# New due times for the keys, the first queries and the logits in an attention-plus-experts kernel

## The chip, the core and the metric

The kernel runs on one core of one Trainium2 chip. The metric is the device time of one execution in microseconds (us), as the median of several runs. TensorE does the matmuls, VectorE and ScalarE read their results out of PSUM, GpSimd takes some subtractions and the indirect transfers, and SyncE's queue issues nearly all DMAs. In the rows of the profile these are PE (PEld for weight loads), DVE, ACT, POOL and SP.

## What is computed

Four batches of 11456 tokens with 128 channels, 49 agents for each batch, and 8 experts of width 1024. Cut to what matters:

```python
def sm(a, b):                                   # softmax over the last axis
    s = scale * (a @ b.transpose(0, 2, 1))
    s = s - s.max(-1, keepdims=True)
    e = np.exp(s)
    return e / (e.sum(-1, keepdims=True) + 1e-09)
agent_v = sm(agents, k) @ v                     # 49 x 128 for each batch
x = sm(q, agents) @ agent_v                     # tokens x 128
logits = x @ w_gate                             # 8 experts
expert_idx = np.argmax(logits, axis=1)
gate = softmax(logits)[expert_idx]
out[t] = gate[t] * (relu(x[t] @ w1[e]) @ w2[e]) # e = expert_idx[t]
```

## The kernel before

A batch is cut into 12 chunks: eleven of 1024 tokens (128 partitions of 8 tokens) and one of 192. Every fp32 operand is split into a high and a low f16 part, so that three f16 matmuls stand for one fp32 matmul.

**The expert work** of a batch is 23 groups of 512 tokens (the last one smaller) by 8 tiles of the hidden width, which makes 184 turns of the generator `experts`, called steps here. A step writes one `ph` tile with two matmuls (`layer1`, lines 1204 and 1205), ScalarE and VectorE turn it into `hh` (lines 1210 and 1211), and five steps later (`LAG`) twelve matmuls of `layer2` (line 1224) read that `hh`. Four `ph` tiles in PSUM let TensorE run ahead of VectorE by a few steps. The first layer reads `M`, the transposed exponentials of a query chunk; 16 steps use one chunk. One expert is chosen for a whole batch (`choose`), and its weights are folded with the agent values into `Ah` and `Al` and split into `w2h` and `w2l` (`weights`, with the small chain of `pow2_scale`, lines 185 to 197). Tokens of other experts are gathered and redone in blocks near the end.

**The attention work** is laid between these steps. For each chunk `prepare` sums squares (line 332), splits the loaded tile into `hl` (ScalarE line 360, VectorE line 362) and lets SyncE issue a DMA transposition into `hT` (line 387). Then
- the keys of the next batch go through `kscores` (lines 415 to 417, ScalarE copies the scores to `S` in line 433) and `kmax` (VectorE `mx`, line 452), all 12 chunks before the values may start;
- the queries of the batch go through `qscores` (VectorE `mq` and `E`, lines 616 and 618), `qexp` (ScalarE, then a store `exps`), `esplit` three steps later (VectorE or GpSimd `mm`, lines 630 and 634), and a DMA transposition into `M` (line 640);
- `logits` (line 649) multiplies `M` by the gating weights, VectorE reduces the result into `Ld` (line 651), and `route` and `factors` make from it the gate that `store` needs.

Scores, logits, values and all small matmuls share two PSUM tiles (`psS`).

**What sets the order.** Each piece of work is an event with a due time in steps, counted from the start of the batch that it belongs to; a heap hands the events out in the order of these times, and the code that they call is written into the program in that order. Each engine then works through its own list in order, and the compiler's tile layer may shift a row by a few places. The due times come from the numbers at the top of the file. `KS` and `KT` are the first key chunk and the steps between chunks: -208 is 24 steps ahead of the batch before (184 steps). `QA` and `QB` do the same for the first three query chunks, `QC` (13 steps) for the rest. `KL` is the distance from preparing a chunk to its scores, `LL` from scores to logits, and `KLL`, `LLL` are these two for the last batch. Step numbers in this document are (batch, step), both from 0. A chunk of keys is named by the batch whose keys they are.

Of the kernel before, what the change touches and what calls it, by code (L numbers as in the profile page):

```python
# [45 lines left out]
KS0, KT0, KL0, VT0, VL0, QS0, QT0, QL0 = -200, 2, 4, 2, 1, -146, 3, 5  # L46
VE, T1, TF0, TF1, TL, TLM, Q0 = 12, 1.75, 3, 1.5, 18, 10, 2

KS, KT, VT, VL, VL4, TW0, TW1, DW = -208, 9, 5.3, 8, 5, 8, 2.5, 1
QA, QB, QC, QB3, KL, LL, UD, RG, D1, DL = -20, 8, 13, 10.5, 9, 9.5, 2, 0.7, 0.5, 0  # L50

KS1 = []

KLL, LLL = 11, 11

DTR, DTE, DEX, DST, DXS = 2, 0.5, 2, 2, 0.5

# [13 lines left out]
def agent_moe_kernel(ctx, tc, q, k, v, agents, wg, w1, w2, out):  # L71
# [185 lines left out]
    def at(t, f, *a):  # L257
        count[0] += 1
        heapq.heappush(events, (t, count[0], f, a))
# [4 lines left out]
    def turns(gen, t, dt, n):  # L264
        for i in range(n):
            at(t + i * dt, next, gen, None)
# [3 lines left out]
    def attention(b):  # L270
        st = state[b]
        base = b * steps
        first, last = b == 0, b + 1 == B
# [492 lines left out]
        def use(t, src, c):  # L766
            uses.append((base + t, b, src, c))

        def prepare(t, src, c):
            at(base + t, squares, src, c)  # L770
            at(base + t + (0 if first else D1), total, src, c)
            at(base + t + (0.5 if first else UD), total2, src, c)
            at(base + t + (1 if first else D1 + 0.3 if src != "v" else UD + 1), transposed if how[src, c] == "C" else split, src, c)
# [6 lines left out]
        for c in range(NCK):  # L780
            t = KS1[c] - base if b == 1 and c < len(KS1) else ks + kt * c
# [8 lines left out]
        for c in range(NCK):  # L790
            t = tv + vt * c
# [21 lines left out]
        for c in range(NCK):  # L813
            if first and c < NQ:
                t, ql_ = QS0 + QT0 * c, QL0
            else:
                t = (Q0 + QC * (c - 3) if first and c > 2 else QA + QB * c if c < 3 else
                     QA + 2 * QB + (QB3 if last else QC) * (c - 2))
                ql_ = KLL if last and c > 2 else KL
            use(t, "q", c)  # L820
            prepare(t, "q", c)
            at(base + t + ql_, qscores, c)
            at(base + t + ql_ + (0 if first and c < NQ else DL), qexp, c)
            at(base + t + ql_ + 3, esplit, c)
            tl = max(t + ql_ + (TL if first and c < NQ else LLL if last and c > 2 else LL), ta + (TLM if first else 4) + c / 2)
            at(base + tl, logits, c)
            if c + 1 in starts or c == NCK - 1:
                turns(route(c), base + tl + 1, RG, 6)
                tf = max(tl + 1 + 6 * RG, tw + 1)
                at(base + tf, factors, c)  # L830
                c0 = max(x for x in starts if x <= c)
                assert tf < c0 * 16 + LAG + 8, (b, c, tf)
# [444 lines left out]
    for b in range(B):  # L1277
        attention(b)
        turns(experts(b), b * steps, 1, steps + LAG + 2)
        turns(leftover_ranks(b), b * steps + (LT3 if b + 1 == B else LT), LTS3 if b + 1 == B else LTS, 6)  # L1280
# [92 lines left out]
```

## Time and profile before

| | |
|---|---|
| three runs | 1165.85, 1166.04 and 1166.94 us, median 1166.04 |
| profiled execution | 1163.97 us |
| its span, first to last instruction | 1162.2 us |
| PE, DVE, ACT, POOL busy | 1028.1, 1016.7, 840.4, 231.5 us |
| mean granted TensorE clock | 0.961 of full speed |

The expert steps run from 85.6 us (the first matmul of line 1204) to 1104.1 us (the last). What stands ahead is the first batch's attention, what follows are the gathered blocks. Batches begin at 85.6, 357.9, 612.9 and 862.9 us. A busy share tells little here, since the two busiest engines wait on each other through four PSUM tiles; what counts is in which step TensorE stands still, for whom, and whether VectorE had work left in that time.

### The profile page before, as it was taken

To read this page: it belongs to the slowest core of one execution; us is meant where nothing else is said; L and a number is where in the kernel's file an instruction comes from. 1 tells how busy PE (TensorE), PEld (TensorE's weight loads), DVE (VectorE), ACT (ScalarE), POOL (GpSimd) and SP (SyncE) were. 2 spreads that over 40 slices of the span, in tenths; PEclk is the share of its full clock that TensorE was granted. 3 is DMA by queue.
4 is the path that set the end of the run, shared out by engine and by line. 5 is a ranking of instruction groups with operands and counts; after the bars stand their busy time and mean duration, and the time that the engine had idled before them with its cause. 6 is when DMAs were issued, how large, how long until landed. Compare 5 with 4: busy or idle time off the path is not lost. (4 is left out here: it accounts for less than half of the span.)

```text
span 1162.2 us, 36038 instructions
## 1 busy us (share of the span) xinstructions
PE 1028.1 (88%) x14607; PEld 827.9 (71%) x14607; DVE 1016.7 (87%) x2407; ACT 840.4 (72%) x1506; POOL 231.5 (20%) x369
## 2 busy tenths in 40 slices
PE   6757789988989989989988889999989988989895
PEld 5645668767867777777776677777767776767795
DVE  7867798889989988998989997999899988899794
ACT  8548786689669787798678885896585555756591
POOL 1301010035400110143300110245100213110133
PEclk9877999999998999999999999999999999999998
DMA  8489999371489899371499898450574544523370
GB/s 331 131 235 215 250 237 203 99 187 59 84 233 268 189 248 223 108 189 47 84 274 267 195 249 184 122 126 32 161 182 104 127 102 102 158 67 112 118 258 14
DMA packets 265673, 191.02 MB, mean 164 GB/s; under 512 B 217513, under 2 KB 230306, under 8 KB 265504
## 3 DMA queue, kind: packets, MB, share of 16 engines
q1 hardware_dynamic: 263648, 185.39, 62.9%
q0 software_dynamic: 1568, 2.25, 1.0%
q8 instruction: 115, 1.88, 0.7%
q10 hardware_dynamic: 288, 1.05, 0.3%
q14 instruction: 54, 0.44, 0.1%
HBM read 99.75 MB, written 36.43 MB: 117 GB/s over the span
## 5 line engine op out<-in xcount | busy, mean ns | idle before, releaser
L1224 PEld LDWEIGHTS <-hh 128*128 128x128 f16 x8640 | 555.4, 100 | 168.9 <-issue 9.8
L1224 PE MATMUL py<-w2h,hh 128*128 128x128 f16 (+1 forms) x5760 | 615.5, 222 | 4.2 <-issue 2.6
L1210 ACT ACTIVATE hh<-ph 128x512 f16<-128x512 f32 (+1 forms) x728 | 411.8, 586 | 183.0 <-PE ph L1205 164.4
L1224 PE MATMUL py<-w2l,hh 128*128 128x128 f16 (+1 forms) x2880 | 531.2, 222 | 0.0
L1211 DVE SCALAR_TENSOR_TENSOR hh<-ph,hh 128x512 f16<-128x512 f32 (+1 forms) x736 | 479.0, 667 | 47.1 <-ACT hh L1210 44.1
L1204 PE MATMUL ph<-M,Ah 128*128 128x512 f16 (+1 forms) x736 | 278.3, 378 | 26.1 <-DVE hh L1211 23.6
L1205 PE MATMUL ph<-M,Al 128*128 128x512 f16 (+1 forms) x736 | 279.0, 380 | 0.1
L362 DVE SCALAR_TENSOR_TENSOR hl<-ld,mul,hl 128x1024 f16<-128x1024 f32 (+1 forms) x120 | 147.7, 1234 | 13.6 <-ACT hl L360 13.1
L332 ACT ACTIVATE jk<-ld 128x1024 f16<-128x1024 f32 (+1 forms) x132 | 133.9, 1014 | 29.9 <-PE pa L734 10.4
L360 ACT ACTIVATE hl<-ld,mul 128x1024 f16<-128x1024 f32 (+1 forms) x120 | 130.7, 1095 | 21.2 <-DVE mul L216 20.4
L219 POOL TENSOR_SCALAR div<-hb,bits 128x1 int32<-128x1 int32 (+1 forms) x96 | 39.9, 425 | 363.5 <-DVE hb L212 312.8
L1205 PEld LDWEIGHTS <-Al 128*128 128x128 f16 x736 | 72.4, 98 | 33.5 <-issue 30.4
L1204 PEld LDWEIGHTS <-Ah 128*128 128x128 f16 x736 | 73.7, 100 | 6.3 <-issue 3.5
L415 PEld LDWEIGHTS <-hT 128*128 128x128 f16 (+1 forms) x630 | 53.2, 98 | 20.3 <-DMA hT<-hl 19.5
L415 PE MATMUL ps_s<-agh,hT 128*128 128x49 f16 x572 | 54.1, 187 | 14.8 <-DMA hT<-hl 11.0
L1237 DVE TENSOR_TENSOR yo<-py,cs 128x512 f32<-128x512 f32 (+1 forms) x92 | 61.3, 666 | 0.2 <-PE py L1224 0.2
L219 POOL TENSOR_SCALAR div<-hb 128x1 int32<-128x1 int32 (+3 forms) x45 | 14.0, 312 | 223.4 <-DVE hb L212 198.0
L416 PE MATMUL ps_s<-agl,hT 128*128 128x49 f16 x572 | 53.8, 186 | 0.0
L417 PE MATMUL ps_s<-agh,hT 128*128 128x49 f16 x572 | 53.7, 186 | 0.0
L416 PEld LDWEIGHTS <-hT 128*128 128x128 f16 (+1 forms) x630 | 52.1, 98 | 2.3 <-issue 1.7
L417 PEld LDWEIGHTS <-hT 128*128 128x128 f16 (+1 forms) x630 | 51.6, 98 | 0.3
L493 POOL TENSOR_TENSOR es<-es,S 128x392 f32<-128x392 f32 (+1 forms) x39 | 41.3, 1060 | 40.3 <-ACT S L483 31.7
(304 smaller groups left out, 1385.9 us busy)
## 6 DMA issues: line engine op xcount, KB each, us to landing
ld<-in_k_dram SPq DMA_DIRECT2D x44, 512.0 KB
ld<-in_v_dram SPq DMA_DIRECT2D x44, 512.0 KB
ld<-in_q_dram SPq DMA_DIRECT2D x44, 512.0 KB
out_dram<-yo SPq DMA_DIRECT2D x88, 256.0 KB
w1e<-in_moe_w_dram SPq DMA_DIRECT2D x17, 512.0 KB
w2e<-in_moe_w_dram SPq DMA_DIRECT2D x17, 512.0 KB
exps<-E SPq DMA_DIRECT2D x44, 196.0 KB
wn<-in_moe_w_dram SPq DMA_DIRECT2D x16, 512.0 KB
```

The source lines that it names most:

```text
L332: nc.scalar.activation(jk[:p, :t * D], x[:p, :t, :].rearrange("p t d -> p (t d)"), AF.Square, accum_out=ss[:p])
L360: nc.scalar.activation(hi[:p, :t, :], x[:p, :t, :], AF.Copy, scale=m)
L362: nc.vector.scalar_tensor_tensor(lo[:p, :t, :], x[:p, :t, :], m, hi[:p, :t, :], op0=ALU.mult, op1=ALU.subtract)
L415: nc.tensor.matmul(o, x[:, 0, i, :p], AG["h"], start=True, stop=False)
L416: nc.tensor.matmul(o, x[:, 0, i, :p], AG["l"], start=False, stop=False)
L417: nc.tensor.matmul(o, x[:, 1, i, :p], AG["h"], start=False, stop=True)
L1204: nc.tensor.matmul(ph[:, :nn], st['Ah'][:, f, :], m, start=True, stop=False)
L1205: nc.tensor.matmul(ph[:, :nn], st['Al'][:, f, :], m, start=False, stop=True)
L1210: nc.scalar.activation(hh[:, 0, :nn], ph[:, :nn], AF.Relu)
L1211: nc.vector.scalar_tensor_tensor(hh[:, 1, :nn], ph[:, :nn], 0.0, hh[:, 0, :nn], op0=ALU.max, op1=ALU.subtract)
L1224: mm_ = lambda l, r, **k: nc.tensor.matmul(o, l, r, skip_group_check=True, **k)
L1237: nc.vector.tensor_tensor(yo[:p, :n, :], py[:p, :n * D].rearrange("p (i d) -> p i d", d=D), cs.unsqueeze(2).broadcast_to([p, n, D]), op=AL ...
```

## The change

It changes numbers of the table, and one expression so that the first batch keeps its old first queries.

```diff
-KS, KT, VT, VL, VL4, TW0, TW1, DW = -208, 9, 5.3, 8, 5, 8, 2.5, 1
-QA, QB, QC, QB3, KL, LL, UD, RG, D1, DL = -20, 8, 13, 10.5, 9, 9.5, 2, 0.7, 0.5, 0
+KS, KT, VT, VL, VL4, TW0, TW1, DW = -214, 9.5, 5.3, 8, 5, 8, 2.5, 1
+QA, QB, QC, QB3, KL, LL, UD, RG, D1, DL = -31, 12, 13, 10.5, 9, 13, 2, 0.7, 0.5, 0
+QA0, QB0 = -20, 8
-KLL, LLL = 11, 11
+KLL, LLL = 11, 13
-                t = (Q0 + QC * (c - 3) if first and c > 2 else QA + QB * c if c < 3 else
+                t = (Q0 + QC * (c - 3) if first and c > 2 else QA0 + QB0 * c if first else QA + QB * c if c < 3 else
```

Worked out into due times, in steps of the batch in which the work is done: the keys of the next batch are prepared at -30, -20.5, -11, -1.5, 8, ... 74.5 where it was -24, -15, -6, 3, 12, ... 75, and their scores follow 9 steps later in both. The queries of batches 1 to 3 are prepared at -31, -19, -7 and then 6, 19, ... where it was -20, -12, -4 and then 9, 22, ... (in the last batch the later ones are 10.5 apart, and 3 steps earlier too). In batch 0 the queries stay. The logits of a chunk come 13 steps after its scores in place of 9.5, in the last batch, from the fourth chunk on, 13 in place of 11. So in batch 0 the logits come 3.5 steps later; in batches 1 and 2 the scores come 3 steps earlier and the logits half a step later, from the third chunk on. The amount of work is the same, and the names of the lines after the table rise by one.

On VectorE, in batch 1 from step 34 to 40, the list before stands like this: from the last writing of a query chunk's `mm` (line 634) to the reading of its logits (line 651), with the `hh` of the steps between.

```order
727 L634 TENSOR_TENSOR mm_141<-E,mm_141 128x8x49
728 L1211 SCALAR_TENSOR_TENSOR hh<-ph,hh 128x512 x2
729 L1237 TENSOR_TENSOR yo<-py,cs 128x512
730 L1211 SCALAR_TENSOR_TENSOR hh<-ph,hh 128x512
731 L362 SCALAR_TENSOR_TENSOR hl<-ld,mul,hl 128x1024
732 L1211 SCALAR_TENSOR_TENSOR hh<-ph,hh 128x512 x2
733 L362 SCALAR_TENSOR_TENSOR hl<-ld,mul,hl 128x1024
734 L452 TENSOR_TENSOR mx<-mx,S 128x392
735 L1211 SCALAR_TENSOR_TENSOR hh<-ph,hh 128x512
736 L651 TENSOR_REDUCE Ld<-ps_s 128x72
```

The same stretch of the changed program:

```order
727 L635 TENSOR_TENSOR mm_141<-E,mm_141 128x8x49
728 L1212 SCALAR_TENSOR_TENSOR hh<-ph,hh 128x512 x3
729 L363 SCALAR_TENSOR_TENSOR hl<-ld,mul,hl 128x1024
730 L1212 SCALAR_TENSOR_TENSOR hh<-ph,hh 128x512 x2
731 L1238 TENSOR_TENSOR yo<-py,cs 128x512
732 L453 TENSOR_TENSOR mx<-mx,S 128x392
733 L1212 SCALAR_TENSOR_TENSOR hh<-ph,hh 128x512
734 L363 SCALAR_TENSOR_TENSOR hl<-ld,mul,hl 128x1024
735 L1212 SCALAR_TENSOR_TENSOR hh<-ph,hh 128x512 x2
736 L363 SCALAR_TENSOR_TENSOR hl<-ld,mul,hl 128x1024
737 L1212 SCALAR_TENSOR_TENSOR hh<-ph,hh 128x512
738 L652 TENSOR_REDUCE Ld<-ps_s 128x72
```

Six steps of `hh` stood between the two, now nine, and one more split of a chunk (`hl`) has come in between.

The second place is VectorE at the end of batch 1, steps 172 to 175, ahead of the scale of the next batch's weights (`pm` and `pdg`, lines 187 and 189, read and fed by the small matmuls of lines 185 and 191). Before:

```order
1059 L1211 SCALAR_TENSOR_TENSOR hh<-ph,hh 128x512
1060 L1237 TENSOR_TENSOR yo<-py,cs 128x512
1061 L1211 SCALAR_TENSOR_TENSOR hh<-ph,hh 128x512
1062 L616 TENSOR_REDUCE mq<-ps_s 128x8
1063 L1211 SCALAR_TENSOR_TENSOR hh<-ph,hh 128x512
1064 L618 TENSOR_TENSOR E<-ps_s,mq 128x392
1065 L187 TENSOR_REDUCE pm<-ps_small 2x1
1066 L1211 SCALAR_TENSOR_TENSOR hh<-ph,hh 128x512
1067 L189 TENSOR_SCALAR pdg<-ident,pm 2x2
```

And in the changed program:

```order
1069 L1212 SCALAR_TENSOR_TENSOR hh<-ph,hh 128x512
1070 L1238 TENSOR_TENSOR yo<-py,cs 128x512
1071 L453 TENSOR_TENSOR mx<-mx,S 128x392
1072 L1212 SCALAR_TENSOR_TENSOR hh<-ph,hh 128x512
1073 L363 SCALAR_TENSOR_TENSOR hl<-ld,mul,hl 128x1024
1074 L1212 SCALAR_TENSOR_TENSOR hh<-ph,hh 128x512
1075 L617 TENSOR_REDUCE mq<-ps_s 128x8
1076 L188 TENSOR_REDUCE pm<-ps_small 2x1
1077 L619 TENSOR_TENSOR E<-ps_s,mq 128x392
1078 L190 TENSOR_SCALAR pdg<-ident,pm 2x2
```

A maximum over keys (`mx`) and a split (`hl`) that stood later have moved in ahead of `pm`, and one `hh` fewer stands between `pm` and `pdg`. On TensorE the matmul of line 191 that waits for `pdg` stood after step 177 in batches 0 and 1 and stands after step 176 now; in batch 2 it stood after 176 and stands after 177. At the start of batch 0, TensorE's scores of the fourth key chunk stood after step 12 and stand after step 8 now, ahead of the fourth query chunk, which stays after step 10.

## Rows read from the trace of the kernel before

**Rows 1.** The page: the mean busy share of the 16 DMA engines, in tenths, in 40 slices of the span (29 us each).

```profile
DMA  8489999371489899371499898450574544523370
```

**Rows 2.** The waits of TensorE over the whole span: who waited, for whom, us in total, times, longest.

```profile
PE ph L1204 <- DVE hh L1211: 23.6, 28, 2.8
PE ps_s L649 <- DMA M<-mm: 17.8, 13, 2.6
PE ps_s L415 <- DMA hT<-hl: 11.0, 6, 4.0
...
PE ps_y L649 <- DMA M<-mm: 4.4, 2, 2.7
```

**Rows 3.** The timeline of batch 0: the first matmul of two steps in a row where nothing is waited for (start, duration).

```profile
119.86 0.38 PE L1204 MATMUL ph<-M,Ah 128*128 128x512 f16 x1
...
120.97 0.38 PE L1204 MATMUL ph<-M,Ah 128*128 128x512 f16 x1
```

**Rows 4.** The timeline around (1,40), of three engines: VectorE writes `mm`, SyncE's queue, and TensorE's logits with its idle time and what ended it.

```profile
407.64 0.56 DVE L634 TENSOR_TENSOR mm<-E,mm 128x392 f16<-128x392 f32 x1
...
406.38 3.65 SPq L387 DMA_TRANSPOSE hT<-hl  x1
410.75 1.79 SPq L640 DMA_TRANSPOSE M<-mm  x1
...
415.63 0.36 PE L649 MATMUL ps_s<-Gs,M 128*128 128x18 f16 x8 [2.65 <-DMA M<-mm]
```

**Rows 5.** Busy time in the 15 stretches that end with a wait of the logits for `M`, each from the logits before it: length, busy us (and instructions) of PE, PEld, DVE, ACT and POOL, granted clock, DMA share, GB/s. The four in which VectorE idled longer than the wait, and the sum of all.

```profile
235.50:257.90 22.40, 18.71 (x271) 14.39 (x267) 20.37 (x41) 19.45 (x36) 7.12 (x9) 0.92 0.76 170
...
415.60:433.40 17.80, 17.54 (x238) 13.96 (x238) 15.06 (x32) 13.17 (x22) 3.52 (x7) 0.90 1.11 234
...
611.80:623.00 11.20, 8.78 (x136) 6.46 (x137) 9.51 (x27) 10.17 (x21) 0.91 (x1) 1.00 1.08 300
648.20:670.40 22.20, 16.80 (x265) 13.33 (x262) 19.71 (x30) 20.22 (x37) 1.25 (x1) 1.00 1.01 216
...
sum 250.20, PE 212.22 PEld 168.29 DVE 235.47 ACT 220.92 POOL 39.48; mean PE 14.15 PEld 11.22 DVE 15.70 ACT 14.73 POOL 2.63
```

**Rows 6.** The timeline of TensorE: the logits that end those four stretches.

```profile
257.93 0.36 PE L649 MATMUL ps_y<-Gs,M 128*128 128x18 f16 x8 [1.73 <-DMA M<-mm]
...
433.44 0.36 PE L649 MATMUL ps_s<-Gs,M 128*128 128x18 f16 x8 [0.27 <-DMA M<-mm]
...
622.96 0.36 PE L649 MATMUL ps_s<-Gs,M 128*128 128x18 f16 x8 [0.69 <-DMA M<-mm]
...
670.44 0.36 PE L649 MATMUL ps_s<-Gs,M 128*128 128x18 f16 x8 [1.58 <-DMA M<-mm]
```

**Rows 7.** VectorE's groups of instructions over the whole span: count | busy us, mean ns of one | idle before, releasers.

```profile
L1211 DVE SCALAR_TENSOR_TENSOR hh<-ph,hh 128x512 f16<-128x512 f32 (+1 forms) x736 | 479.0, 667 | 47.1 <-ACT hh L1210 44.1
L362 DVE SCALAR_TENSOR_TENSOR hl<-ld,mul,hl 128x1024 f16<-128x1024 f32 (+1 forms) x120 | 147.7, 1234 | 13.6 <-ACT hl L360 13.1
...
L452 DVE TENSOR_TENSOR mx<-mx,S 128x392 f32<-128x392 f32 (+1 forms) x44 | 23.4, 531 | 6.5 <-ACT S L433 6.2 <-issue 0.2
...
L618 DVE TENSOR_TENSOR E<-ps_s,mq 128x392 f32<-128x392 f32 (+1 forms) x40 | 21.3, 532 | 0.2
```

**Rows 8.** TensorE alone in five stretches of 3.4 us and their granted clock (length, busy, clock, DMA share, GB/s), and the matmul of line 1204 with its wait inside the first and at the start of the fifth.

```profile
139.80:143.20 3.40, 3.03 (x17) 0.50 1.09 313
170.50:173.90 3.40, 3.40 (x40) 0.50 0.96 277
...
416.20:419.60 3.40, 3.40 (x28) 0.51 0.92 230
522.10:525.50 3.40, 3.40 (x43) 0.50 0.68 242
...
935.10:938.50 3.40, 3.40 (x27) 0.50 0.52 81
...
140.17 0.59 PE L1204 MATMUL ph<-M,Ah 128*128 128x512 f16 x1 [2.43 <-DVE hh L1211]
...
934.75 0.38 PE L1204 MATMUL ph<-M,Ah 128*128 128x512 f16 x1 [2.83 <-DVE hh L1211]
```

**Rows 9.** TensorE's waits in batches 1 and 2 (357.9 to 862.9 us), same columns as Rows 2.

```profile
PE ps_s L415 <- DMA hT<-hl: 5.1, 4, 1.7
```

**Rows 10.** The ends of batches 0, 1 and 2, from step 156 on: busy time with the columns of Rows 5, and the matmul of line 191 with its wait in batches 0 and 2.

```profile
570.80:612.90 42.10, 37.56 (x516) 30.46 (x514) 37.52 (x109) 29.76 (x54) 2.47 (x10) 0.96 0.91 229
...
823.90:862.90 39.00, 34.19 (x467) 27.67 (x464) 33.42 (x98) 27.97 (x51) 1.68 (x5) 1.00 0.73 204
316.20:357.90 41.70, 38.51 (x516) 31.82 (x514) 36.51 (x109) 29.95 (x54) 2.49 (x10) 0.92 0.88 245
...
348.50 0.55 PE L191 MATMUL ps_small<-pdg,ones 2*128 2x2 f32 x2 [2.33 <-DVE hb L212]
...
854.21 0.35 PE L191 MATMUL ps_small<-pdg,ones 2*128 2x2 f32 x2 [2.70 <-DVE pdg L189]
```

**Rows 11.** The start of batch 0: SyncE's issues of the transpositions of the fourth query chunk and of the fourth key chunk, and TensorE's first score matmul of that key chunk.

```profile
102.97 1.94 SPq L387 DMA_TRANSPOSE hT<-hl  x1
...
106.55 4.31 SPq L387 DMA_TRANSPOSE hT<-hl  x1
...
114.48 0.19 PE L415 MATMUL ps_s<-agh,hT 128*128 128x49 f16 x1
```

## The prediction

> **What bounds the kernel now.** I read the page first, then the waits of TensorE, then for each kind of wait the stretch that leads to it. The expert steps fill 1019 of the 1162.2 us, so a gain has to come from there or from the start of batch 0. A step that waits for nothing takes 1.10 us (120.97 − 119.86) [rows 3], so TensorE is the bound wherever it doesn't stand still, and the question is for whom it stands. Over the span it waited 23.6 us in 28 places for VectorE's `hh`, 17.8 + 4.4 = 22.2 us in 15 places for the transposed exponentials `M` at the logits, and 11.0 us in 6 places for the transposed queries or keys `hT` [rows 2]. The change moves the work around the last two; it takes no instruction away.
>
> What a wait for `M` is made of shows best at (1,40). VectorE had `mm` ready at 408.20 (407.64 + 0.56). SyncE's queue was then issuing a transposition into `hT` from 406.38 for 3.65 us, so that of `M` was issued only at 410.75, and the logits began at 415.63, 2.65 us after TensorE was ready for them [rows 4]. The transfer is late because of a queue and of busy DMA engines (seven to nine tenths in most slices of batches 0 to 2 [rows 1]). The logits stand in TensorE's list where they come too early.
>
> Next comes what VectorE did in those stretches, since a TensorE that waits lets VectorE catch up. From the preceding logits to the late ones, all 15 together: 250.20 us, with VectorE busy for 235.47 [rows 5]. It idled 14.7 us, less than the 22.2 us that TensorE waited. So part of the wait was used by VectorE to work off what it would otherwise be waited for. That decides how much comes back.
>
> **The logits later.** The nine and a half steps from scores to logits become thirteen, 3.5 × 1.10 = 3.85 us more in batches 0 to 2, and two steps, 2.2 us, in the last. The longest wait is 2.7 us [rows 2], and the ones in the last batch are under that. So every one of the 15 waits has its cover, as long as the transfers start no later than now; the order shows six steps of `hh` between the writing of `mm` and the reading of the logits before, and nine now. What each wait gives back is bounded by VectorE's idle time in its own stretch. In eleven stretches the idle time is taken up to the wait, no more; in the four shown VectorE idled longer than the wait: 22.40 − 20.37 = 2.03 against 1.73, 17.80 − 15.06 = 2.74 against 0.27, 11.20 − 9.51 = 1.69 against 0.69, 22.20 − 19.71 = 2.49 against 1.58 [rows 5, 6]. Of the 14.73 us of idle time those surpluses (0.30 + 2.47 + 1.00 + 0.91 = 4.68) are no use to a wait, so **10.1 us** come back at once. The other 12.1 us would turn into waits for `hh`, unless VectorE has less to do there. Lower bound 5 us (half of the idle time is of use, if it lies ahead of work that wasn't ready), upper bound 22.2.
>
> **VectorE's load moved.** Between steps 0 and 75 of each of batches 0 to 2 nine chunks of the next batch's keys are prepared now, eight after the change: one moves to the end of the batch before. With it go one whole split `hl`, 1.234 us, and one maximum `mx`, 0.531 [rows 7], so 1.77 us. This is the part of the batch in which the waits for `M` lie (all but four of the 15 before step 70). In batches 1 and 2 it is given back to the 12.1 us above: 2 × 1.77 = **3.5 us** (bounds 0 and, with the rest as well, 12.1). In batch 0 the chunk moves into the opening, and is counted below. The sum of returned waits is 13.6 us of 22.2.
>
> **The clock.** After three of the waits for `M`, and only after these of the 15, TensorE ran at a granted clock of 0.50 to 0.51 of full speed (1.2 in place of 2.4 GHz) for 3.4 us, at 170.5, 416.2 and 522.1 [rows 8]. At half speed 1.7 us of each are lost, 5.1 in all. But the same 3.4 us at 0.50 stand behind waits for VectorE: one of 2.43 us at 140.17 and one of 2.83 at 934.75 [rows 8]. A wait that only changes its name keeps the slow stretch. I take half, **2.5 us** (0 to 5.1).
>
> The Trainium skill, page "TensorE: Matmul & The Clock Gate", section "Loop structure matters more than you think", has it that work of VectorE on PSUM between matmuls doesn't take the warm clock away. By that all 5.1 us would come back, even where VectorE becomes what is waited for, and the sum would be 2.6 us lower. The two stretches behind VectorE's waits speak against it here, and the sum goes by them.
>
> **The scores of queries earlier.** The waits for `hT` in batches 1 and 2 are 5.1 us in 4 places [rows 9]. Their queries are prepared 3 to 11 steps earlier, but their scores, 9 steps behind, move as well; what helps is only the more even spacing (12 steps between the first three queries in place of 8) and one key transposition fewer in those steps. I take **2 us** (0 to 5.1).
>
> **The ends of batches.** Here the change costs. Ahead of `pdg`, for which TensorE's small matmul of line 191 waits, one `mx` and one `hl` more stand in VectorE's list, and one `hh` fewer: 1.234 + 0.531 − 0.667 = 1.10 us later [rows 7]. TensorE's matmul meanwhile stands one step earlier in batches 0 and 1, 1.10 us. So its wait, 2.33 us in batch 0 [rows 10], would grow by 2.2 us there, in both batches **4.4 us**. VectorE idled some 5 us in the last 39 to 42 us of each of these batches (41.70 − 36.51 = 5.2, 42.10 − 37.52 = 4.6, 39.00 − 33.42 = 5.6 [rows 10]), so nothing is lost but at this one place. In batch 2 the matmul stands one step later, which pays for the 1.10: 0. Bounds: 0 (the idle time takes it all, since four `ph` tiles let TensorE run ahead) and 8 (three ends, worked out under the rivals).
>
> **The start of batch 0.** One more key chunk is prepared before the first step, and the fourth chunk's scores now stand after step 8 in place of 12, ahead of the fourth query's. Its transposition was issued at 106.55 for 4.31 us and its scores ran at 114.48 without a wait; the query's transposition was issued ahead of it at 102.97, 1.94 us [rows 11]. Four steps earlier the scores would stand at 114.48 − 4.4 = 110.1, and 106.55 + 4.31 = 110.86 is only the end of the issue, so SyncE's order must have moved with it. I take the nearest: 0.8 us of waiting and 0.7 for the order of the two, **1.5 us** lost (0 to 4, the longest `hT` wait [rows 2]).
>
> **Two PSUM tiles for scores and logits.** The logits' new place brings some of them next to the scores of a following chunk, and both take turns in `psS`. Nothing in the trace prices this alone; I take 0, with −2 (a conflict goes) and +3 (one more wait as long as the longest for `hh`, 2.8 [rows 2]).
>
> **The sum.** 10.1 + 3.5 + 2.5 + 2.0 − 4.4 − 1.5 = 12.2 us gained. From the profiled 1163.97 that is 1151.8; the profiled execution lies 2.1 us below the median of 1166.04, which all runs hold within 0.2 to 0.9 us, so I set the sum against the median: 1153.8, and forecast **1154**. With the terms' bounds most likely to go together (a return of 8 to 18 us with clock, costs of 3 to 8) it is 1146 to 1161.
>
> **Rivals.**
> 1. *The waits only change their names.* The 14.7 us of idle time were not usable, and VectorE, moved by nothing but one chunk, lets TensorE wait for `hh` in place of `M`. For it speaks that VectorE was busy for 235.47 of 250.20 us there [rows 5]; against it that TensorE ran at 1.10 a step between [rows 3]. The return is 5 + 1, the ends cost 4: 1161 to 1167. Chance 0.15.
> 2. *The batch ends decide, slower.* If VectorE runs without idle time up to `pdg`, the shift counts in all three batches with the exponentials `E` ahead of the small chain's end as well: 1.234 + 0.531 + 0.532 [rows 7], with what waits behind it some 2.7 us each, 8 us, and each wait grown beyond 2.43 us can bring a half-clock stretch of 1.7 us [rows 8], 5 us. With 4 us at the start of batch 0 this is 17 against a return of 10: 1173. It decides from about 4 us for each end on. For it speaks that line 191 already waits 2.33 and 2.70 us [rows 10]; against it the 5 us of idle VectorE in each of these stretches. Chance 0.14.
> 3. *All comes back.* If VectorE's work, freed of the chunk, spreads itself in the gaps, 22.2 of waits, 5.1 of clock and 3 of `hT` return, against 4 to 6 of costs: 1166 − 30 + 5 = 1141. Against it VectorE's 94% in those stretches. Chance 0.06.
>
> That the due times don't reach the lists is excluded by the order printed above.
>
> **How the numbers follow.** The forecast has 0.65. A measurement of this kernel can tell some 0.2% from no change, so "same" is 1163.7 to 1168.4. The forecast and rival 3 are faster, rival 1 is faster in a third of its cases: 0.65 + 0.06 + 0.04 = 0.75. Same: 0.11. Slower: rival 2, 0.14. The range reaches from the forecast's own low end, 1145, over rival 1 to 1168; what is left out is rivals 2 and 3, 0.20.
>
> **What would show it.** Right: the logits' 15 waits for `M` are under 4 us together; waits for `hh` grow from 23.6 by some 8 us; no half clock at 416 and 522; line 191 waits near 4.5 us in batches 0 and 1. Batch 0 should be shorter by 3 us, batches 1 and 2 by some 5 each, the last by about 1 or none. Rival 1 shows `hh` waits above 35 us; rival 2 longer stretches from step 156 to the end and waits of 4 to 5 us at line 191 with half clock behind them. The prediction is wrong if `M` still comes late at thirteen steps (its issue on SyncE is then later than before), or if the scores wait for `hT` longer than 11 us.

## The result, and the profile after

The changed kernel takes 1186.45 us as the median of four runs (1183.99 to 1188.16), where the kernel before takes 1166.49 beside it. The ratio is 1.0148, with a 95% interval of 1.0114 to 1.0182. It is slower by 20 us, where 12 us less were forecast. The profiled execution has a span of 1186.4 us against 1162.2. One run of the kernel before, on a later chip, took 1438.78 us at a granted clock of 0.663 of full speed, and is in no ratio below.

TensorE's waits over the whole span, of the changed kernel, with the columns of [rows 2] (line numbers are one higher):

```profile
PE ph L1205 <- DVE hh L1212: 50.2, 49, 4.0
PE ps_s L416 <- DMA hT<-hl: 14.7, 8, 4.3
...
PE ps_s L650 <- DMA M<-mm: 6.6, 6, 3.1
...
PE ps_small L192 <- DVE hb L213: 4.1, 2, 2.1
...
PE ps_y L650 <- DMA M<-mm: 1.6, 1, 1.6
```

Against [rows 2] the waits for `M` went from 22.2 us in 15 places to 8.2 in 7. The prediction had all 15 covered, under 4 us together, and 13.6 us of them returned as time. A wait that is gone is not yet time returned, so the 14.0 us that went are no measure of these 13.6. Line 192's longest wait is 2.1 us and not 4.5. But TensorE now waits 50.2 us for `hh` in place of 23.6. That is 26.6 us more, while VectorE's busy time rose by only 4.7 us (1021.4 against 1016.7) in a span that is 24 us longer. VectorE is not full; it waits too. One engine further back stands ScalarE, whose waits the prediction never looked at. ScalarE's waits over the whole span, of the kernel before:

```profile
ACT jk L332 <- DMA ld<-in_q_dram: 8.0, 4, 2.7
...
ACT jk L332 <- DMA ld<-in_k_dram: 6.5, 4, 3.0
```

and of the changed kernel:

```profile
ACT jk L333 <- DMA ld<-in_q_dram: 31.2, 10, 10.3
...
ACT jk L333 <- DMA ld<-in_k_dram: 14.2, 9, 3.5
ACT jk L929 <- DMA wn<-in_moe_w_dram: 12.5, 2, 6.7
```

`jk` is the sum of squares with which the work on a loaded tile begins. It needs the load, and it stands in ScalarE's list ahead of the activations that make `hh`. Within the expert steps, summed over the waits of over 0.15 us, ScalarE waits 12.2 us for loads in the kernel before and 46.6 us in the changed one (the longest `q` wait, 10.3 us, lies ahead of the first step and is not counted).

Where the 23.5 us between the last steps (1104.1 and 1127.6) come from, stretch by stretch: steps 0 to 127 of batches 0 to 3 give −12.1, −2.5, +2.9 and +4.3; steps 128 to 155 of the first three batches +6.2, +7.1 and +4.0; steps 156 to 183 of these +4.9, +4.9 and +4.3; the rest of the last batch −1.3 and the start +0.8. So batch 0 gained 12 us at first, and the 28 steps ahead of a batch's last 28 cost more than these. Busy time in steps 128 to 155 of batches 0, 1 and 2, columns of [rows 5], of the kernel before:

```profile
280.00:316.17 36.17, 34.44 (x521) 27.69 (x519) 33.64 (x74) 27.33 (x49) 18.36 (x34) 1.00 0.25 53
534.55:570.76 36.21, 35.08 (x523) 27.88 (x521) 33.84 (x74) 27.31 (x50) 16.91 (x35) 1.00 0.24 59
788.34:823.85 35.51, 34.70 (x523) 27.75 (x521) 32.80 (x70) 23.78 (x43) 17.62 (x35) 1.00 0.22 56
```

and of the changed kernel, with steps 156 to 183 of the three batches behind them, which answer to [rows 10]:

```profile
268.66:311.03 42.37, 35.86 (x532) 28.40 (x530) 34.39 (x80) 26.01 (x48) 20.04 (x37) 1.00 0.28 62
531.81:575.15 43.34, 36.06 (x532) 28.49 (x530) 36.38 (x80) 26.19 (x48) 18.32 (x37) 1.00 0.28 62
800.50:840.01 39.51, 35.39 (x529) 28.08 (x527) 36.98 (x76) 26.68 (x47) 18.06 (x37) 1.00 0.20 49
311.03:357.59 46.56, 36.63 (x527) 29.18 (x527) 38.80 (x115) 33.80 (x61) 2.46 (x7) 1.00 0.86 219
575.15:622.15 47.00, 39.59 (x527) 31.89 (x527) 38.75 (x114) 33.93 (x61) 2.72 (x8) 0.93 0.90 215
840.01:883.37 43.36, 38.52 (x491) 31.43 (x487) 36.29 (x106) 27.69 (x50) 0.79 (x2) 0.88 0.68 180
```

In the first two stretches TensorE and VectorE both idle for 6 to 8 us, where TensorE idled 1 to 2 and VectorE 2.5 before. Neither is full, so at least part of the time is lost in a chain of waits. One such chain, ahead of (1,156): the timeline of SyncE's queue, ScalarE, VectorE and TensorE in the changed kernel.

```profile
562.29 6.00 SPq L388 DMA_TRANSPOSE hT<-hl  x2
...
568.35 0.58 SPq L924 DMA_DIRECT2D wn<-in_moe_w_dram  x1
...
572.74 1.06 ACT L929 ACTIVATE jk<-wn 128x1024 f16<-128x1024 f32 x1 [6.66 <-DMA wn<-in_moe_w_dram]
...
573.80 1.06 ACT L1211 ACTIVATE hh<-ph 128x512 f16<-128x512 f32 x2
574.41 1.29 DVE L1212 SCALAR_TENSOR_TENSOR hh<-ph,hh 128x512 f16<-128x512 f32 x2 [4.87 <-ACT hh L1211]
575.15 0.38 PE L1205 MATMUL ph<-M,Ah 128*128 128x512 f16 x1 [3.19 <-DVE hh L1212]
```

`wn` is a load of expert weights whose squares are summed at fixed steps; six of them belong to each of batches 0 and 1. The code gives it the two buffers of the transposed keys (tag `hTk`). The last one is due at step 158. In the kernel before, it stands in SyncE's list ahead of the next batch's first transpositions, and was issued at 522.66. Now it stands behind two of them: by their due times that of the first query chunk, prepared 11 steps earlier than before, and that of the first key chunk, 6 steps earlier. SyncE's queue first stood 9.1 us until VectorE had the split `hl` ready, and the two then took 6.00 us. First the load in the kernel before, then that wait of SyncE's queue in the changed kernel, between 545 and 580 us, with the columns of [rows 2]:

```profile
522.66 0.34 SPq L923 DMA_DIRECT2D wn<-in_moe_w_dram  x1
...
SPq L388 <- DVE hl L363: 9.1, 1, 9.1
```

ScalarE stands 6.66 us, VectorE 4.87 and TensorE 3.19. At (2,58) a chain of the same kind hangs on the load of a query chunk:

```profile
693.28 6.85 SPq L388 DMA_TRANSPOSE hT<-hl  x2
...
700.18 0.57 SPq L288 DMA_DIRECT2D ld<-in_q_dram  x1
...
704.14 6.92 SPq L388 DMA_TRANSPOSE hT<-hl  x1
704.15 0.42 ACT L333 ACTIVATE jk<-ld 96x256 f16<-96x256 f32 x1 [4.81 <-DMA ld<-in_q_dram]
...
706.95 0.58 PE L1205 MATMUL ph<-M,Ah 128*128 128x512 f16 x1 [4.04 <-DVE hh L1212]
```

### The profile page after: what moved, and what is told of

The parts are those of the page before. It is cut to its first block, busy times and chain, and to the rows that moved or that the text cites. A ratio compares the mean times of both kernels' runs of the same rounds, so it can differ in the third digit from the quotient of the medians.

```text
span 1186.4 us, 36017 instructions
## 1 busy us (share of the span) xinstructions
PE 1031.3 (87%) x14607; PEld 827.9 (70%) x14607; DVE 1021.4 (86%) x2407; ACT 840.0 (71%) x1506; POOL 228.7 (19%) x369
## 5 line engine op out<-in xcount | busy, mean ns | idle before, releaser
L1225 PEld LDWEIGHTS <-hh 128*128 128x128 f16 x8640 | 554.2, 100 | 171.3 <-issue 11.3
L1205 PE MATMUL ph<-M,Ah 128*128 128x512 f16 (+1 forms) x736 | 279.1, 380 | 54.7 <-DVE hh L1212 50.2
L333 ACT ACTIVATE jk<-ld 128x1024 f16<-128x1024 f32 x132 | 133.5, 1011 | 50.8 <-DMA ld<-in_q_dram 31.2
L416 PE MATMUL ps_s<-agh,hT 128*128 128x49 f16 x588 | 54.2, 185 | 15.4 <-DMA hT<-hl 14.7
L416 PEld LDWEIGHTS <-hT 128*128 128x128 f16 (+1 forms) x630 | 51.8, 98 | 21.0 <-DMA hT<-hl 20.4
L417 PEld LDWEIGHTS <-hT 128*128 128x128 f16 (+1 forms) x630 | 50.6, 97 | 1.6 <-issue 1.3
L418 PEld LDWEIGHTS <-hT 128*128 128x128 f16 (+1 forms) x630 | 50.5, 97 | 0.1
```

Of the source, the lines that this page charges most:

```text
L333: nc.scalar.activation(jk[:p, :t * D], x[:p, :t, :].rearrange("p t d -> p (t d)"), AF.Square, accum_out=ss[:p])
L416: nc.tensor.matmul(o, x[:, 0, i, :p], AG["h"], start=True, stop=False)
L417: nc.tensor.matmul(o, x[:, 0, i, :p], AG["l"], start=False, stop=False)
L418: nc.tensor.matmul(o, x[:, 1, i, :p], AG["h"], start=False, stop=True)
L1205: nc.tensor.matmul(ph[:, :nn], st['Ah'][:, f, :], m, start=True, stop=False)
L1225: mm_ = lambda l, r, **k: nc.tensor.matmul(o, l, r, skip_group_check=True, **k)
```

## The experiments

All ratios are to the kernel before, with their 95% intervals. On the later chips the kernel before was itself less even than above (medians of 1171 to 1174 us, runs from 1162.57 to 1182.63), so each ratio is of runs on one chip, and differences under 0.3% are not read. The changed kernel itself was not run again there: where a ratio is set against its 1.0148, two ratios of different chips are compared. Growth of a stretch of steps and sums of waits are from one profiled execution of each kernel, set against that of the kernel before with its 1163.97 us. That one is among its fastest, and some of the others are the slowest of their kernel (1196.59 us with a median of 1190.23 for the middle keys). So a stretch that differs by 2 or 3 us shows little, and the stretches of an experiment add up to more than its ratio says, by some 10 us in most.

**The three parts apart.** Keys alone:

```diff
-KS, KT, VT, VL, VL4, TW0, TW1, DW = -208, 9, 5.3, 8, 5, 8, 2.5, 1
+KS, KT, VT, VL, VL4, TW0, TW1, DW = -214, 9.5, 5.3, 8, 5, 8, 2.5, 1
```

> Only the key numbers are changed (-214 and 9.5), queries and logits as before. Theory A (the early keys do the harm at the ends of batches: the first key transposition of the next batch takes one of the two buffers that it shares with the last load of the expert weights for their squares, that load comes late and ScalarE stands 6 us at its square in batches 0 and 1): 1170 to 1178 us, with a wait of ScalarE for wn of over 4 us near step 155 of batches 0 and 1. Rival B (the later logits do the harm): within 3 us of the kernel before. Rival C (the early queries do it): within 3 us of the kernel before, and no wait for wn.

Measured: 1.0275 (1.0234 to 1.0317). The keys alone lose nearly twice what the whole change loses. ScalarE waits 4.4 and 4.5 us for `wn`. But the waits for `M` also rise, to 24.5 us at `ps_s` (17.8 before) and 4.0 at line 1204 (none before), and the loss is beyond theory A's range, so that theory named only part of it. The longest wait for `M` is at (0,46), where TensorE waits 6.80 us:

```profile
157.04 8.34 SPq L387 DMA_TRANSPOSE hT<-hl  x2
159.78 0.91 POOL L634 TENSOR_TENSOR mm<-E,mm 128x392 f16<-128x392 f32 x1 [10.02 <-ACT hh L1210]
...
166.59 1.23 SPq L640 DMA_TRANSPOSE M<-mm  x1
...
171.38 0.39 PE L649 MATMUL ps_s<-Gs,M 128*128 128x18 f16 x8 [6.80 <-DMA M<-mm]
```

`mm` is ready at 160.69, and its transposition is issued at 166.59, behind two others that hold the queue for 8.34 us.

Queries alone (`QA`, `QB` and the expression, keys and logits as before):

> Only the first queries and what follows from them are moved (-31, 12 apart), keys and logits as before. Theory A: one query chunk more in the last 30 steps of a batch costs 2 to 3 us in each of three, 1165 to 1175. Rival B: no change, 1163 to 1169. Rival C (the queries are nearly all of the loss): 1180 or more.

Measured: 1.0012 (0.9984 to 1.0039), no change that can be told. The ranges of theory A and of rival B both hold it, rival C is out. Queries and logits, with `KS, KT` as before:

> The changed kernel with the keys as before (-208, 9). Theory A: most of the loss is gone, the waits for M stay gone: 1158 to 1168, and no wait of ScalarE for wn. Rival B or C: 1180 to 1188, as the changed kernel.

Measured: 0.9987 (0.9955 to 1.0018). Without the keys the loss is gone, ScalarE waits for no `wn`, and rivals B and C fall. But ScalarE's waits for loads in the expert steps are 32.3 us in this kernel, 12.2 in the kernel before, and nothing is lost by them. Keys and queries, with the logits as before (`LL` 9.5, `LLL` 11):

> The changed kernel with the logits as before (9.5 and 11). Theory A: the waits for M are back (10 to 15 us) on top of the changed kernel: 1186 to 1200. Rival B: 1162 to 1170.

Measured: 1.0274 (1.0233 to 1.0314), waits for `M` of 30.1 us in 13 places at `ps_s`. With the logits later it was 1.0148: beside the new keys the later logits are worth 1.3%, some 15 us.

**Logits alone.**

```diff
-QA, QB, QC, QB3, KL, LL, UD, RG, D1, DL = -20, 8, 13, 10.5, 9, 9.5, 2, 0.7, 0.5, 0
+QA, QB, QC, QB3, KL, LL, UD, RG, D1, DL = -20, 8, 13, 10.5, 9, 11.5, 2, 0.7, 0.5, 0
-KLL, LLL = 11, 11
+KLL, LLL = 11, 13
```

> The kernel before with the logits alone later: 11.5 steps past the scores in place of 9.5 (13 in the last batch in place of 11); thirteen does not fit beside the queries' old times. The step of the prediction on the logits alone: 2.2 us more of cover, the waits for M fall from 22 to under 8 us, and 6 to 12 us come back, ratio 0.990 to 0.995. Rival I (the time goes into waits for hh): waits for M fall as much, ratio 0.997 to 1.002.

Measured: 0.9939 (0.9906 to 0.9971). The waits for `M` fall from 22.2 to 7.2 us (5.4 at the logits, 1.8 at line 1204), and 0.61% of the time, 7 us against these 15, comes back; the waits for `hh` rise from 23.6 to 31.1 and those for `hT` at `ps_s` from 11.0 to 19.1. So the term was right in kind, and about half of the waits that went only changed their names.

**The loads.** The loads of the expert weights 8 steps earlier, and loads of chunks five uses ahead, each alone and together in the changed kernel, and the second in the kernel before:

```diff
-LT, LTS, LT3, LTS3, N0, NTT, NDL = 144, 6, 121, 5, -56, 6, 4
+LT, LTS, LT3, LTS3, N0, NTT, NDL = 144, 6, 121, 5, -64, 6, 4
...
-AHEAD = 3
+AHEAD = 5
```

> The changed kernel with the loads of the expert weights for their squares 8 steps earlier (-64 in place of -56), so that the last of them is issued ahead of the next batch's first key transposition. Theory A (that load costs TensorE 3.0 and 3.2 us at the ends of batches 0 and 1): 6 to 8 us less than the changed kernel, a ratio to the kernel before of 1.007 to 1.011, and no wait of ScalarE for wn over 1 us. Rival D (the wait only gives way to another, since VectorE has as much to do there): within 2 us of the changed kernel, ratio 1.014 to 1.018.

Measured: 1.0048 (1.0016 to 1.0080), no wait for `wn`. The gain is larger than expected, and most of it isn't where the wait was: against the changed kernel steps 128 to 183 of batches 0 and 1 are 5.1 and 0.0 us shorter (steps 128 to 155 alone 2.0 and 0.5), but steps 0 to 63 of batches 1 and 2 are 6.9 and 7.5 us shorter, where no such load stands. So the late `wn` explains little of what steps 128 to 155 lost, and the way to the later gain is not shown.

> The changed kernel with the loads of keys, values and queries issued five uses ahead in place of three. Theory E (the common cause: ScalarE, in order, stands at the squares of a chunk whose load is issued late, behind transpositions in SyncE's queue; 33 us of such waits in the expert steps of the changed kernel that the kernel before didn't have): the waits of ScalarE for ld in q, k and v in the expert steps fall from 33 to under 12 us, and the time by 8 to 15 us: ratio 1.002 to 1.010. Rival F (the DMA engines are full, so that a load issued earlier makes a transposition late): waits for hT and M grow by as much, ratio 1.012 to 1.020.

Measured: 1.0039 (1.0012 to 1.0066). ScalarE's waits for chunks in the expert steps fall from 34.1 to 19.4 us, not under 12, and the gain of 1.1% is as theory E had it.

> Both of these edits in the changed kernel. Theories A and E: the sums add, 14 to 22 us less than the changed kernel, ratio 0.996 to 1.004. Rivals D and F: ratio 1.012 to 1.020.

Measured: 0.9896 (0.9838 to 0.9954), faster than both kernels. ScalarE's waits for loads in the steps are down to 16.6 us. The two edits together give back 2.5%, which the interval doesn't tell apart from the sum of each, 2.1%.

> The kernel before with loads five uses ahead, as a control. Theory E: its ScalarE waits for such loads are 12 us only, so it gains 0 to 5 us: ratio 0.995 to 1.000. Rival F: slower by 2 us or more, ratio over 1.002.

Measured: 0.9946 (0.9912 to 0.9980). Theory E had 0.995 to 1.000. The time lies a little below that, and the reason doesn't hold here: ScalarE's waits for loads stay at 13.6 us against 12.2, and TensorE's waits for `M` even rise from 22.2 to 34.2 us while the time falls. Where the 0.5% comes from is not shown; a sum of waits is no price.

The loads of the expert weights 6 steps later in the kernel before (`N0` −50):

> The kernel before with the loads of the expert weights for their squares 6 steps later (-50 in place of -56), so that the last of them is issued behind the next batch's first key transposition. Theory A: ScalarE waits 4 to 7 us for wn near the end of batches 0 and 1, TensorE 3 us in each, ratio 1.003 to 1.008. Rival D: such a wait, but ratio within 0.998 to 1.002.

Measured: 1.0168 (1.0130 to 1.0206). ScalarE waits 7.9 us for `wn` in two places, as expected; but the loss is twice what was expected. Steps 156 to 183 of batches 0 and 1 grow by 3.1 and 5.2 us, steps 0 to 127 of batches 1 and 2 by 8.6 and 7.6. So it, too, does most of its harm later.

**The values, half a step.** Where the values begin is worked out from `KS` and `KT`: −214 + 11 × 9.5 is −109.5, and −208 + 11 × 9 is −109. So the change moves the values of the next batch half a step earlier, and with them the choice of its expert and the making of its weights, which the diff doesn't show. (It also moves the work on the next batch's agents 6 steps earlier, since that hangs on `KS` as well.) That half step alone, in the kernel before:

```diff
-        tk = ks + kt * (NCK - 1) + kl + 2
+        tk = ks + kt * (NCK - 1) + kl + (2 if first else 1.5)
```

> The kernel before with nothing changed but the values of the next batch (from the maximum of the keys on) half a step earlier, as they stand in the changed kernel. Theory G: steps 128 to 156 grow from 36 by 2 to 6 us in each of batches 0 to 2, ratio 1.004 to 1.015. Rival H: within 0.3% of the kernel before.

Measured: 1.0134 (1.0096 to 1.0172). Steps 128 to 155 grow by 2.0, 2.7 and 3.4 us; more of the loss lies in the other stretches, and TensorE's waits for `hh` rise from 23.6 to 37.6. Taken back in the changed kernel (2.5 in place of 2 after the first batch):

> The changed kernel with only the next batch's values put back half a step later, where they stood before the change. Theory G (the unnoticed half step of the values, by itself 1.013 in the kernel before, carries the loss in the changed kernel too): ratio 0.998 to 1.006. Rival H (in the changed kernel the keys at the batch ends carry it, and the half step counts only in the kernel before): ratio 1.010 to 1.018.

Measured: 1.0071 (1.0031 to 1.0110), between the two theories: about half of the loss. ScalarE's waits for `wn` fall with it, from 12.5 to 3.3 us, so the half step and the late load are not two separate costs. Steps 128 to 155 of the three batches, for comparison with 42.37, 43.34 and 39.51:

```profile
269.88:309.97 40.09, 35.57 (x525) 28.18 (x523) 36.96 (x82) 25.16 (x45) 18.42 (x37) 1.00 0.28 57
529.07:567.87 38.80, 35.95 (x526) 28.29 (x524) 36.72 (x79) 25.09 (x46) 19.06 (x37) 1.00 0.23 53
789.39:826.57 37.18, 35.31 (x524) 27.98 (x522) 35.38 (x71) 25.81 (x46) 17.00 (x36) 1.00 0.22 52
```

That is 9.1 of the 17.3 us that these stretches had lost. The same in the changed kernel with earlier loads, and in the one with the new keys alone:

> The changed kernel with loads five uses ahead and the weights' loads 8 steps earlier, and with the values of the next batch half a step later, where they stood in the kernel before. Theory G (steps 128 to 156 of batches 0 to 2 are 4 to 5 us longer than before because the values now meet the batch's last queries' route half a step off): these three stretches fall from 40.0, 41.4 and 39.9 us to under 38 each and the time by 5 to 12 us, a ratio of 0.980 to 0.986. Rival H (it is the denser work at the ends itself: keys 30 steps ahead): within 2 us, ratio 0.987 to 0.992.

Measured: 0.9966 (0.9936 to 0.9996), no better than 0.9896 without it and outside both ranges. Theory G fails here: whether the half step counts hangs on what else is in the list.

> The key numbers alone (-214, 9.5) in the kernel before, with the values where they stood. Theory G: the keys alone cost 1.0275 with the half step, and 1.010 to 1.017 without it. Rival H: 1.022 to 1.030.

Measured: 1.0262 (1.0228 to 1.0297), rival H. The keys lose by themselves.

**The keys in two parts.** The first four chunks at their new times, with the agents 6 steps earlier as in the change, or the other eight alone; all else as before. The first of the two, without its lines on the agents (the second has `c > 3`):

```diff
...
+            if not first and c < 4:
+                t = -214 + 9.5 * c
```

> The kernel before with only the first four key chunks of the next batch at their new times (-30, -20.5, -11, -1.5, and the agents 6 steps earlier with them); the other eight, the values, the queries and the logits as before. If the ends of batches carry the loss of the new keys: steps 156 to 184 grow by 4 to 8 us each, ScalarE waits for wn, ratio 1.010 to 1.018. If the collision of the later keys with M on SyncE's queue carries it: ratio 1.000 to 1.006.

Measured: 1.0225 (1.0184 to 1.0265), more than expected. Steps 156 to 183 of batches 0 and 1 grow by 6.0 and 4.8 us, ScalarE waits 10.8 us for `wn` in two places, and steps 0 to 63 of batches 1 and 2 grow by 7.2 and 11.8 us. The agents were not moved apart from these chunks.

> The kernel before with only the fifth to the twelfth key chunk at their new times (8 to 74.5, 9.5 apart); the first four, the values, the queries and the logits as before. If their collision with the transposition of M carries the loss: waits for M of over 5 us near step 46 of batch 0, steps 0 to 64 grow by 4 to 9 us in each batch, ratio 1.008 to 1.018. If the ends carry it: ratio 0.998 to 1.005.

Measured: 1.0146 (1.0105 to 1.0188). Steps 0 to 63 of batches 1 and 2 grow by 14.1 and 11.3 us; those of batch 0 don't (−1.2), and no wait for `M` is over 5 us, though both had been expected. The waits of TensorE over the whole span, to be held against [rows 2]:

```profile
PE ps_s L649 <- DMA M<-mm: 28.4, 12, 4.8
PE ps_s L415 <- DMA hT<-hl: 24.9, 11, 4.4
```

At (1,53):

```profile
440.62 5.24 SPq L387 DMA_TRANSPOSE hT<-hl  x1
441.01 1.82 POOL L634 TENSOR_TENSOR mm<-E,mm 128x392 f16<-128x392 f32 x1 [5.88 <-ACT hl L360]
...
446.57 1.23 SPq L640 DMA_TRANSPOSE M<-mm  x1
...
451.00 0.38 PE L649 MATMUL ps_s<-Gs,M 128*128 128x18 f16 x8 [4.81 <-DMA M<-mm]
```

Both halves of the keys lose, and by different waits: with the early ones ScalarE waits for loads at the ends of batches (and more is lost behind that), with the middle ones transpositions of keys stand ahead of that of `M`. ScalarE's waits for loads are 9.6 us with the middle keys, less than the 12.2 of the kernel before, so that loss doesn't come by them.

**Faster versions.**

> The kernel before with the logits 11.5 steps past the scores (13 in the last batch) and loads five uses ahead. If the two gains (0.9939 and 0.9946) are of separate waits, ratio 0.986 to 0.991; if loads further ahead only pay where the ends are dense, 0.992 to 0.996.

Measured: 0.9898 (0.9860 to 0.9936): as if the two gains add (0.9939 × 0.9946 = 0.9885), and no key or query has to move.

> The changed kernel with the keys as before and loads five uses ahead. Theory E (32 us of ScalarE's waits for loads in the expert steps of that kernel): 8 to 15 us less than without it, ratio 0.986 to 0.992. Rival F: ratio 0.995 to 1.002.

Measured: 0.9991 (0.9969 to 1.0014), rival F. ScalarE's waits for loads fall from 32.3 to 19.6 us and the time doesn't. A ScalarE wait on a load is thus not by itself a loss; theory E fits where the ends are dense with the new keys, and not as a rule.

## Why the prediction was wrong

**The step that failed: the ends of batches** (4.4 us at line 191). It was wrong in place and in size. Line 192's wait is 2.1 us where it was 2.3. Steps 128 to 183 of batches 0 to 2 cost 17.3 + 14.1 = 31.4 us, and more than half of that lies ahead of step 156, where the prediction's stretches began. The runs show what brings it: the new keys, since without them the loss is gone (0.9987) and alone they lose 2.8%, 2.6 with the values put back. How it comes about is shown in part. The half step of the values is 9.1 us of the 17.3, as taken back. The late `wn` holds TensorE 3.02 and 3.19 us ahead of (0,156) and (1,156), but with the load issued earlier steps 128 to 155 got back only 2.0 and 0.5. The prediction wrote that VectorE's 5 us of idle time there would cover all but one place, and it priced what VectorE's list alone gains and loses; ScalarE's waits were not read at all. Ahead of (1,156) VectorE itself stood 4.87 us for ScalarE, and its idle time covered nothing.

**The key chunk moved out of steps 0 to 75** ("given back", 3.5 us) was wrong as well. It counted two VectorE instructions, and left out that the transpositions of the other eight chunks move against that of `M` on SyncE's queue. Moved alone, those eight cost 1.5%, 17 us. The keys alone lengthen steps 0 to 63 of batches 1 and 2 (by 9.1 and 9.6 us with the values put back). Beside all the new keys the later logits are worth 1.3% (1.0274 without them, 1.0148 with them), so part of their gain went into waits that the change itself brings; how much is not shown, since the eight chunks and the later logits were not run together without the rest.

**The waits for M** (10.1 us): right in kind. Logits alone gained 0.6%, 7 us, at 11.5 steps. In the changed kernel 8.2 us of waits for `M` remain, and the longest, 3.05 us at (1,53), is longer than any before, so thirteen steps were no full cover. Both signs of being wrong that the prediction had named came: `M` still late, and 14.7 us of waits of the scores for `hT`, over 11. That batch 0's first 128 steps are 12.1 us shorter, where 3 were forecast for the whole batch, is no proof of the term: its waits for `M` there fell by 4.1 us (6.3 to 2.3), and TensorE's busy time fell by 4.3 us with the same number of matmuls, because less of it ran at the lower clock (granted 0.93 and 1.00 in the two halves of these steps, where it was 0.89 and 0.98).

**The half step of the values** had no term. The prediction priced the keys, the queries and the logits, whose numbers stand in the diff; `tk`, where the values begin, isn't in the diff and depends on two of them.

**The waits for hT in batches 1 and 2** (−2): wrong in sign. 5.1 us in 4 places [rows 9] became 10.2:

```profile
PE ps_s L416 <- DMA hT<-hl: 10.2, 6, 2.6
```

**The clock** (2.5 us gained): the three stretches at half speed behind waits for `M` are gone, as forecast, but a new one stands behind the longest wait for `M` (the second line has the columns of [rows 8]):

```profile
432.19 0.36 PE L650 MATMUL ps_s<-Gs,M 128*128 128x18 f16 x8 [3.05 <-DMA M<-mm]
...
432.40:435.80 3.40, 3.40 (x46) 0.50 1.16 265
```

Others came behind waits for `hh`: from 575 us on, and from 705 to 712. Over the expert steps the time lost to the lower level (1.2 GHz, granted 0.50) is 27.1 us before and 24.5 after. That is nearly the forecast, by luck: the stretches that came and went are others than the ones it counted. By the Trainium skill, page "TensorE: Matmul & The Clock Gate", section "Loop structure matters more than you think", a copy by VectorE out of PSUM doesn't break the warm clock, in a loop whose next matmuls follow at once. This trace shows the other case, in which TensorE waits for VectorE: 4.04 us for `hh` at 706.95, and the clock was 0.50 in the stretch from 706.9 to 710.3.

**The start of batch 0** (+1.5): +0.8 ahead of the first step, and with 7.9 us more in steps 0 to 7 and 9.0 less in the next eight, no loss.

**Rival 2** had the right side, but its size (1173, 7 us of the 20) and its place (line 191) were wrong. Rival 1's sign, waits for `hh` above 35 us, came (50.2), with a time outside its range.

**What stays open**: most of the chain by which the new keys lose at the ends of batches; why small shifts at a batch's end do most of their harm in the first 64 steps of the next one (weights 6 steps late, four keys early, and the reverse with the weights 8 steps early). Which row of SyncE's list decides was not tried.

## What to carry to other kernels

Where a program is one fixed order on in-order engines, follow each wait one engine further back, to the engine that everybody waits for and to the queue that issues its loads, before pricing an edit by the busy time of the engine that is named. Work out every due time that hangs on a changed number, not only those that the diff shows, and set the moved transfers beside those that already stand in the issuing queue. Here a half-step shift cost more than a per cent, so the sum of the instructions moved was no guide even to the sign. What gained was more slack (later use and, in most mixes, earlier loads), not moved work. And a wait named in a trace is a place to test, not a price: waits for `M` fell by 15 us for a gain of 7, and rose by 12 in a kernel that got faster.

## What was not expected of the hardware

Issuing one transposition into `hT` held SyncE's queue for 6.92 us at 704.14 in the changed kernel, and two for 8.34 us with the new keys alone, where the one at 102.97 took 1.94 [rows 11]; a load that stands behind them in the queue is issued only after that (the one at 700.18 behind two from 693.28 on). What makes one issue three times as long as another was not tried. And a stretch grew by 7.1 us with no engine full in it (36.06 of 43.34 us busy on TensorE, 36.38 on VectorE, 26.19 on ScalarE).
